# Two chained MLPs behind a Fourier transform: the first MLP cut into blocks of 512, 512 and 482 token pairs instead of 376

## The chip, the core and the metric

One core of a Trainium2 chip runs one program in one launch. The metric is the time of one execution on the device in microseconds (us). The kernel before takes 953.21 us, the median of three runs that lie between 952.99 and 953.53 us.

The core has five engines with a queue each, worked off in order: PE (TensorE) multiplies matrices and adds up in PSUM, DVE (VectorE) and POOL (GpSimd) do elementwise work, ACT (ScalarE) does functions and copies, and SP issues the DMA transfers between the core's memory and HBM. An instruction waits until semaphores say that its inputs are there and its output's buffer is free.

## The reference

```
x: (2, 3008, 256)
a = real(fft(fft(x, axis=1), axis=2))          # real part of the 2-D transform
a = a.reshape(6016, 256)
h = a @ moe_w_in                               # (256, 2048)
a = max(h, 0)**2 @ moe_w_out                   # (2048, 256)
h = a @ moe2_w_in
out = (h * sigmoid(1.702 * h)) @ moe2_w_out
```

All of it is in float32.

## The kernel before

**Token pairs.** The transform of real data gives token k and token 3008 - k almost the same inputs: one is the sum and the other the difference of an even and an odd part. The kernel works on pairs of tokens. Each batch has 1506 pairs, in four parts of frequencies of 378, 376, 376 and 376 pairs (`WID`); the kernel calls them `kb` 0 to 3.

**Words in two halves.** Every float32 matrix of the two MLPs is held as a high half and a low half in a shorter format (`float32r`), and a product is three matmuls: high by high, low by high, high by low. So each operand passes through a cast (high half, ACT, `H` or `h`) and a subtraction (low half, POOL or DVE, `G` or `l`). The weights come as 64-bit words and pass through six or seven integer and float operations first (operations i0A to u3l).

**The start.** The input arrives in six pieces f0 to f5 (three per batch). A piece is folded on DVE (`a`, `s`, `p`, `m`, `u`), goes through the transform over features on PE (`E`, `O`; lines 567 to 577, called L575 in the profile), is copied out by ACT (`e0`, `e1`, `o`), and the transform over positions makes from three pieces the four parts of a batch: `e00`, `e01` (even frequencies) and `o0` (the two odd parts) on PE at L624. PE is kept running with 24 matmuls on zeros (`WARM`, L469) before the first piece is there.

**The first MLP** runs over 8 blocks, one per part and batch, by 16 slices of 128 hidden units: 128 steps. A step i has five operations. `F` (L748 to L750): six matmuls into PSUM, for the even and the odd half. `P` (L1038 to L1041): three DVE instructions that form the two tokens of each pair and add the middle feature. `R` (L1049, L1050): relu and square, two ACT instructions, or one on DVE. `H` (L1055): the high half on ACT. `G` (L212): the low half on POOL or DVE. `B` (L763): twelve matmuls that add to four PSUM tiles, two per output half `ec` and token of the pair. So a step has 18 matmuls, each as wide as the block (376 or 378 columns). `X` takes a partial result out of PSUM to HBM and `Y` brings it back, since the first three blocks are worked in turns while the weights still arrive (`turns`, L733).

**The second MLP** runs over six blocks of 512, 512, 512, 512, 512 and 452 pairs, by 8 units of two slices: 48 units. The product with the first weight is done with seven products of half matrices in place of eight (21 matmuls, L1094), and the second with 24 (L1110): 45 matmuls in a unit. Its inputs come back from HBM (`load_y`); a block of 512 is put together from two or three blocks of the first MLP.

**Order.** The order of the operations up to the end of the first MLP is written out in `ORDER`, a list of names; what engine does an operation that may go to several is in `HOME`, and which buffer of a ring it takes in `RINGS`. The second MLP is written as a loop (L1119 to L1193) with `products`, `back2` and `leave`. After it, the last PSUM tile is copied out by ACT (L1198) and DVE (L1200), each half with its own DMA.

**Rings.** `LAG` (L736) is the number of steps whose `B` is left for the second MLP's first units. The rings of the first MLP hold 5 tiles `h`, 5 `gh`, 4 `gl` and 2 `p`.

Of the kernel before, what the change touches and what calls it, by code (L numbers as in the profile page):

```python
# [44 lines left out]
F4 H2 P4 o0s0 o0E1 o0c1
F5 u0l G1 R3 o0s1 P5 H3 R4 u1A i1S o02h
F6 B0 P6 i1O R5 B1 u1L R6 H4 G2 G3 H5 B2 i2D o02l u1C G4
F7 i1P o02N H6 o02n P7 G5 B3
F8 X3.0 P8 R7 X3.1 i1M u1O
F9 u2D i1N B4 P9 R8  # L50
F10 H7 i1H B5 H8
F11 G6 R9 P10 G7 i1l P11 u1S G8 R10 H9 B6
F12 G9 H10 f3D B7
F13 G10 R11 X7.0 P12 u1P i2A X7.1 R12 H11 u1H i2C
F14 G11 i2L B8 u1l H12 P13 B9 G12 R13 B10 u2A
F15 i2O B11 H13 P14 i2S
F16 R14 P15 i2P
F17 G13 H14 P16 i3D B12 R15 H15 G14 R16 P17
F18 i2M B13 R17 G15
F19 P18 u2C B14 H16 B15 i2N H17 G16 i2H R18 G17 i2l P19 u2L H18 R19 X15.1 X15.0 i3A  # L60
# [1271 lines left out]
```

## Time and profile before

| | |
|---|---|
| median of three runs | 953.21 us |
| the profiled execution: time, span of its records | 953.02 us, 950.8 us |
| PE busy | 942.8 us (99% of the span) |
| DVE, ACT, POOL busy | 686.0, 588.8, 280.2 us |
| HBM read and written | 37.36 MB and 15.42 MB |

The span is the time from the first to the last record; what lies around it in that execution is 2.2 us. Matmuls are pipelined: one shows some 335 ns from start to end while the next begins after about half of that. So the price of a matmul in a stream is read from the starts of two matmuls and the number between them, not from its duration.

### The profile page before, as it was taken

The numbers are of one execution on the slowest core, as the hardware profiler recorded it, in microseconds if no ns is written. First come the engines' busy times: TensorE is split into PE (matmuls) and PEld (weight loads), VectorE is DVE, ScalarE is ACT, GpSimd is POOL, SyncE is SP. The second block draws the span as 40 slices with busy tenths as digits, with TensorE's granted clock in tenths as the row PEclk, the third lists the DMA queues.
The fourth block names the chain that finished last, engine by engine and source line by source line (L and its number), as shares of the span: only waits on it lengthen the run. The fifth ranks groups of instructions, "written<-read, shape, count | busy, mean of one in ns | idle before, by whom it ended". The sixth has DMA issues, their size and how long they took to land.

```text
span 950.8 us, 12392 instructions
## 1 busy us (share of the span) xinstructions
PE 942.8 (99%) x4844; PEld 849.8 (89%) x4844; DVE 686.0 (72%) x902; ACT 588.8 (62%) x699; POOL 280.2 (29%) x171
## 2 busy tenths in 40 slices
PE   8999999999999999999999999999999999999997
PEld 8799999999999899999888888888888888888996
DVE  6899999887887787778797755665575575556553
ACT  3999997858587467867765644644454454455443
POOL 0655674424463367377105110030030002000000
PEclk9999999999999999999999999999999999999999
DMA  7442504221021010020330110020011001000001
GB/s 286 139 166 77 204 34 151 94 66 70 1 77 45 34 45 33 1 70 8 105 105 1 45 45 0 1 89 1 1 45 44 1 19 66 1 1 22 23 1 40
DMA packets 21898, 53.58 MB, mean 56 GB/s; under 512 B 3280, under 2 KB 15184, under 8 KB 19152
## 3 DMA queue, kind: packets, MB, share of 16 engines
q1 hardware_dynamic: 21840, 52.79, 15.8%
q8 instruction: 38, 0.62, 0.3%
q14 instruction: 20, 0.16, 0.1%
HBM read 37.36 MB, written 15.42 MB: 56 GB/s over the span
## 4 chain that ended last, share of the span: by engine, by line
PE 95%; DVE 2%; DMA 1%; ACT 1%; POOL 1%; issue 0%; SPq 0%; DVEq 0%; POOLq 0%
PE psb L763 27%; PE psb L1110 27%; PE psc L1094 24%; PE psa L748 4%; PE psa L749 4%; PE psa L750 4%; PE psa L624 2%; PE psb L624 1%; PE psa L575 1%; DMA xt<-in_x 1%; POOL gl L212 0%; PE psb L575 0%; DVE t L516 0%; DVE t L512 0%; DVE gl L212 0%
## 5 line engine op out<-in xcount | busy, mean ns | idle before, releaser
L763 PE MATMUL psb<-gh,w 128*128 128x376 f32 (+1 forms) x1024 | 233.6, 335 | 0.0
L212 POOL TENSOR_TENSOR gl<-h,gh 128x752 fp32r<-128x752 f32 (+1 forms) x91 | 176.7, 1949 | 161.1 <-ACT gh L1055 73.7
L763 PEld LDWEIGHTS psb<-gh,w 128*128 128x128 f32 x1024 | 181.6, 189 | 1.9 <-issue 1.2
L1110 PE MATMUL psb<-gh,w 128*128 128x512 f32 (+1 forms) x576 | 163.7, 386 | 0.0
L1174 DVE TENSOR_TENSOR g<-u,psc 128x1024 f32<-128x1024 f32 (+1 forms) x48 | 57.5, 1199 | 116.3 <-PE psc L1094 116.3
L1055 ACT CAST gh<-h 128x752 fp32r<-128x752 f32 (+1 forms) x128 | 103.1, 818 | 45.1 <-PE psb L763 44.3
L763 PE MATMUL psb<-gl,w 128*128 128x376 f32 (+1 forms) x512 | 129.8, 334 | 0.0
L1176 ACT ACTIVATE g<-g 128x1536 f32<-128x1536 f32 (+1 forms) x48 | 70.4, 1467 | 94.1 <-DVE g L1174 94.1
L1110 PEld LDWEIGHTS psb<-gh,w 128*128 128x128 f32 x576 | 108.1, 188 | 20.6
L212 DVE TENSOR_TENSOR gl<-g,gh 128x2048 fp32r<-128x2048 f32 (+1 forms) x48 | 109.0, 2270 | 1.5 <-ACT gh L1151 1.5
L1049 ACT ACTIVATE h<-h 128x752 f32<-128x752 f32 (+1 forms) x110 | 91.4, 831 | 21.7 <-DVE h L1041 19.7
L879 POOL TENSOR_TENSOR ue<-raw 128x512 f32<-128x512 f32 (+1 forms) x12 | 24.2, 2037 | 255.0 <-DMA raw<-ydram 248.7
L1050 ACT ACTIVATE h<-h 128x752 f32<-128x752 f32 (+1 forms) x110 | 91.9, 836 | 3.5
L1040 DVE TENSOR_TENSOR h<-p,psa 128x376 f32<-128x376 f32 (+1 forms) x128 | 70.0, 547 | 33.3 <-POOL gl L212 16.1
L763 PEld LDWEIGHTS psb<-gl,w 128*128 128x128 f32 x512 | 92.5, 188 | 0.0
L1038 DVE SCALAR_TENSOR_TENSOR p<-n,w1n_t,psa 128x376 f32<-128x376 f32 (+1 forms) x128 | 76.8, 600 | 20.2 <-PE psa L750 20.0
L1151 ACT CAST gh<-g 128x2048 fp32r<-128x2048 f32 (+1 forms) x48 | 90.2, 1878 | 0.3 <-ACT g L1176 0.3
L1110 PE MATMUL psb<-gl,w 128*128 128x512 f32 (+1 forms) x288 | 87.7, 386 | 0.0
L748 PE MATMUL psa<-eo,w 128*128 128x376 f32 (+1 forms) x256 | 86.4, 338 | 0.3 <-DVE n L306 0.3
L749 PE MATMUL psa<-eo,w 128*128 128x376 f32 (+1 forms) x256 | 85.7, 335 | 0.0
L750 PE MATMUL psa<-eo,w 128*128 128x376 f32 (+1 forms) x256 | 85.4, 334 | 0.0
L1173 ACT ACTIVATE g<-psc 128x512 f32<-128x512 f32 (+1 forms) x48 | 28.4, 591 | 77.7 <-PE psc L1094 77.7
(165 smaller groups left out, 1527.1 us busy)
## 6 DMA issues: line engine op xcount, KB each, us to landing
ydram<-o SPq DMA_DIRECT2D x17, 376.0 KB, 2.9
xt<-in_x SPq DMA_DIRECT2D x5, 1024.0 KB, 7.1
out<-o SPq DMA_DIRECT2D x10, 512.0 KB, 2.6
cst<-in_dfts SPq DMA_DIRECT2D x8, 570.0 KB, 6.0
raw<-in_w1i SPq DMA_DIRECT2D x4, 1024.0 KB, 5.0
raw<-in_w1o SPq DMA_DIRECT2D x4, 1024.0 KB, 6.2
raw<-in_w2i SPq DMA_DIRECT2D x4, 1024.0 KB, 5.3
raw<-in_w2o SPq DMA_DIRECT2D x4, 1024.0 KB, 5.1
```

Source lines behind the costliest of these rows:

```text
L212: eng.tensor_tensor(out=o, in0=a, in1=f32(b), op=ALU.subtract)
L748: T.matmul(o, lhsT=w[:, 0, fs], rhs=t[:, par, 0, 0:wd], start=True, stop=False)
L749: T.matmul(o, lhsT=w[:, 0, fs], rhs=t[:, par, 1, 0:wd], start=False, stop=False)
L750: T.matmul(o, lhsT=w[:, 1, fs], rhs=t[:, par, 0, 0:wd], start=False, stop=True)
L763: T.matmul(acc[j][ec][:, s, 0:wd], lhsT=w[:, hl, e0:e0 + P], rhs=(gh, gl)[gi][:, s, 0:wd], start=(first and hl == 0 and gi == 0), stop=(la ...
L1038: V.scalar_tensor_tensor(out=p[:, 0:wd], in0=e128[blocks[j]][:, 0:wd], scalar=w1n_t[:, 0, f:f + 1], in1=ps[:, 0, 0:wd], op0=ALU.mult, op1= ...
L1049: A.activation(out=hv, in_=hv, func=AF.Relu)
L1050: A.activation(out=hv, in_=hv, func=AF.Square)
L1055: A.copy(st["gh"][:, :, 0:wd], st["h"][:, :, 0:wd])
L1094: T.matmul(bank, lhsT=w[:, hl, slot * P:(slot + 1) * P], rhs=x[:, yl, 0:wd], start=(first and hl == 0 and yl == 0), stop=(hl == 1), skip_g ...
L1110: T.matmul(o[:, s, 0:wd], lhsT=w[:, hl, e0:e0 + P], rhs=g[:, 2 * i + s, 0:wd], start=(f == 0 and hl == 0 and g is gh), stop=(f == 15 and h ...
L1151: A.copy(gh, gs[u - 1])
```

## The change

What it does, part by part.

1. The 1506 pairs of a batch are cut into three blocks of 512, 512 and 482 (`WB`), whatever part they come from. The first MLP has 6 blocks and 96 steps. Block 0 holds part 0 and 134 pairs of part 1; block 1 the other 242 of part 1 and 270 of part 2; block 2 the other 106 of part 2 and part 3. So `h`, `l`, `m`, `n` of parts that are cut write two tiles (`e01hb`, `o02lb`, ...).
2. The second MLP has the same six blocks, 512, 512, 482 twice, and loads each with one DMA.
3. `LAG` is 3 and not 4; the rings hold 4 `h`, 4 `gh`, 3 `gl`. `ORDER`, `HOME` and `RINGS` are new.
4. The first input piece comes in two halves that are each contiguous, and is folded and transformed by halves (`f0p`, `f0pb`, `part_half`). The negated feature constants are no longer loaded, but made by ACT.
5. In the second MLP's last unit the matmuls on low halves stand last for the first output half, and for the second one all of token 0 stand before all of token 1. The last copies are three: token 0 by ACT, token 1 by DVE (240 columns) and ACT (242), into tiles and DMAs of their own.

```
-NP = 378
+NP = 512
+WB = [512, 512, 482]
...
-ORDER = """
-f0D dfD f0a1 f0a0 f0s0 nD f0p f0E f0s1 nyD seD ny f1D f0m f1s0 f2D f1a0 i0D f0e1 nA f1m f0O u0D c00D f1p f0o nC f1u i0A
...
+f0D nyD ny f0Db dfD f0a0 f0s0 f0p f1D nD f0m df f0a1 f0s1 f0pb f0E f0mb f2D f0O f1a0 i0D f1s0 u0D f1p f0Ob f1m f0Eb f1u
...
+TURNS = [(0, 0, 4), (1, 0, 4), (2, 0, 8), (1, 4, 12), (0, 4, 16), (1, 12, 16), (2, 8, 16)] + [(j, 0, 16) for j in range(3, 6)]
-PAIRS = B * sum(WID)
-WID2 = [min(NP2, PAIRS - NP2 * m) for m in range(BLKS)]
+WID2 = B * WB
...
-        nc.sync.dma_start(consts["dft"], dftd.rearrange("p (s l) -> p s l", s=2))
+        nc.sync.dma_start(consts["dft"][:, 0], dftd)
+
+    @op("df")
+    def _():
+        A.mul(consts["dft"][:, 1], consts["dft"][:, 0], -1.0)
...
+        def part_half(par, half):
...
+            for s, of_s in enumerate(slots()):
+                o = ps[:, s // 2, (s % 2) * 130:(s % 2) * 130 + 130] if par == 0 else ps[:, 0, s * P:(s + 1) * P]
+                for i, (v, j, minus, at) in enumerate(of_s):
+                    if at == half:
+                        T.matmul(o, lhsT=v[:, par, j], rhs=consts["dft"][:, minus, cols],
+                                 start=(not half and i == 0 and s in ((0, 2) if par == 0 else (0,))),
+                                 stop=(i == len(of_s) - 1), skip_group_check=True)
...
+    def block_parts(kb):
+
+        at = sum(WID[:kb])
+        for i in range(NC):
+            lo, hi = max(at, NP * i), min(at + WID[kb], NP * i + WB[i])
+            if lo < hi:
+                yield i, lo - at, hi - at, lo - NP * i
...
-    LAG = 4
+    LAG = 3
...
-        return [m.tile([P, 2, NP], F32, **of("h", 5), name="ht") for _ in range(2)]
+        return [m.tile([P, 2, NP], F32, **of("h", 4), name="ht") for _ in range(2)]
...
-        for j, lo, hi, at in pieces(m):
-            nc.sync.dma_start(yr[m][:, :, :, at:at + hi - lo], ydram[j][:, :, :, lo:hi])
+        nc.sync.dma_start(yr[m][:, :, :, 0:WID2[m]], ydram[m][:, :, :, 0:WID2[m]])
...
-            st["gh"] = mg.tile([P, 2, NP], F32R, **of("gh", 5), name="gh")
+            st["gh"] = mg.tile([P, 2, NP], F32R, **of("gh", 4), name="gh")
...
-            gl = mg.tile([P, 2, NP], F32R, **of("gl", 4), name="gl")
+            gl = mg.tile([P, 2, NP], F32R, **of("gl", 3), name="gl")
...
+        terms = [(i, hl, g, s) for i in range(2) for hl, g in ((0, gh), (0, gl), (1, gh)) for s in range(2)]
+        if u == units - 1:
+            terms.sort(key=(lambda x: x[3]) if ec else (lambda x: x[2] is gl))
...
-        A.copy(o[:, 0, 0:wd], acc["2", BLKS - 1][1][:, 0, 0:wd])
-        nc.sync.dma_start(out[BLKS - 1, 1, :, 0, 0:wd], o[:, 0, 0:wd])
-        V.tensor_copy(o[:, 1, 0:wd], acc["2", BLKS - 1][1][:, 1, 0:wd])
-        nc.sync.dma_start(out[BLKS - 1, 1, :, 1, 0:wd], o[:, 1, 0:wd])
+        at = wd // 4 * 2
+        o1, o2 = (m2.tile([P, NP2], F32, tag=tag, name="o") for tag in ("a1", "u"))
+        for eng, to, s, lo, hi in ((A, o1, 0, 0, wd), (V, o2, 1, 0, at), (A, o[:, 0], 1, at, wd)):
+            copy(eng, to[:, lo:hi], acc["2", BLKS - 1][1][:, s, lo:hi])
+            nc.sync.dma_start(out[BLKS - 1, 1, :, s, lo:hi], to[:, lo:hi])
```

Three places of the new order, on the engines themselves. The first is PE's queue ahead of the first MLP step: `psa` and `psb` are PSUM tiles, `zc` and `zs` the transformed pieces, `cst` the constants of positions, `eo` the block that a step reads. Before, from the transform for part 0 to the first step:

```order
22 L624 MATMUL psa<-cst,zs 128x189
23 L624 MATMUL psa<-cst,zs 128x189 [waits Activation_49]
24 L624 MATMUL psa<-cst,zs 128x189 x2
25 L624 MATMUL psb<-cst,zc 128x189 x4
26 L624 MATMUL psb<-cst,zc 128x188 [waits DMAHW3_49,PE_49]
27 L624 MATMUL psb<-cst,zc 128x188 x3
28 L624 MATMUL psb<-cst,zs 128x188 x4
29 L748 MATMUL psa<-eo,w 128x378 [waits Activation_49]
30 L749 MATMUL psa<-eo,w 128x378 [waits DVE_49]
```

And in the changed kernel:

```order
24 L644 MATMUL psa<-cst,zs 128x189
25 L644 MATMUL psa<-cst,zs 128x189 [waits Activation_49] x2
26 L644 MATMUL psa<-cst,zs 128x189
27 L644 MATMUL psb<-cst,zc 128x188 [waits DMAHW3_49,PE_49]
28 L644 MATMUL psb<-cst,zc 128x188 x3
29 L644 MATMUL psb<-cst,zs 128x188 x4
30 L644 MATMUL psb<-cst,zc 128x188 x4
31 L644 MATMUL psb<-cst,zc 128x189 [waits DVE_49,Activation_49]
32 L644 MATMUL psb<-cst,zc 128x189 x3
33 L771 MATMUL psa<-eo,w 128x512 [waits Activation_49]
34 L772 MATMUL psa<-eo,w 128x512 [waits DVE_49]
```

The middle feature of part 1 (four matmuls, row 30) has come ahead of the first step, and that of part 0 (rows 31 and 32) behind part 1, where it waits for DVE and ACT to free a PSUM tile.

The second place is ACT's queue at the same time: `zc` and `zs` are the copies `e0`, `e1`, `o`, and `ue` is a weight on its way. Before:

```order
14 L596 ACTIVATE zc<-psa,nyq 128x65 [waits PE_49]
15 L596 ACTIVATE zc<-psa,nyq 128x65 x3
16 L497 CAST sel_t<-sel_raw 128x128
17 L306 COPY zs<-psb 128x512
18 L596 ACTIVATE zc<-psa,nyq 128x65 x4
19 L596 ACTIVATE zc<-psa,nyq 128x65 [waits PE_49]
20 L596 ACTIVATE zc<-psa,nyq 128x65 x3
21 L306 COPY zs<-psb 128x512 [waits PE_49]
22 L319 ACTIVATE ue<-raw 128x1024 [waits DMAHW1_49,DVE_49]
```

And in the changed kernel:

```order
15 L598 ACTIVATE zc<-psa,nyq 128x65 [waits PE_49]
16 L598 ACTIVATE zc<-psa,nyq 128x65 x3
17 L289 ACTIVATE ue<-raw 128x1024 [waits DMAHW2_49,DMAHW0_49,DVE_49]
18 L598 ACTIVATE zc<-psa,nyq 128x65 [waits PE_49]
19 L598 ACTIVATE zc<-psa,nyq 128x65 x7
20 L467 COPY mask<-sel_raw 128x1 [waits DMAHW2_49]
21 L471 CAST sel_t<-sel_raw 128x128
22 L276 COPY zs<-psb 128x512 [waits PE_49]
23 L276 COPY zs<-psb 128x512
24 L295 ACTIVATE ue<-raw 128x1024
```

A conversion of a weight (row 17) has come between the copies of the third piece, and both `zs` copies stand at the end.

The third place is the end of the program, ACT and DVE. ACT before, its last five instructions:

```order
670 L1173 ACTIVATE g<-psc 128x452 [waits DVE_49,PE_49]
671 L1176 ACTIVATE g<-g 128x3x452 [waits DVE_49]
672 L1151 CAST gh<-g 128x4x452 [waits PE_49,Activation_49]
673 L1116 COPY o<-psb 128x2x452 [waits DMAHW1_49,DMAHW0_49,PE_49]
674 L1198 COPY o<-psb 128x452 [waits DVE_49,PE_49]
```

ACT in the changed kernel:

```order
604 L1188 ACTIVATE g<-g 128x3x482 [waits DVE_49]
605 L1163 CAST gh<-g 128x4x482 [waits PE_49,Activation_49]
606 L1128 COPY o<-psb 128x2x482 [waits DMAHW6_49,DMAHW5_49,PE_49]
607 L276 COPY o<-psb 128x482 [waits PE_49]
608 L276 COPY o<-psb 128x242 [waits DVE_49]
```

DVE in the changed kernel:

```order
793 L1155 TENSOR_TENSOR g<-g,psc 128x482 [waits DVE_49]
794 L1186 TENSOR_TENSOR g<-u,psc 128x2x482 [waits PE_49]
795 L180 TENSOR_TENSOR gl<-g,gh 128x4x482 [waits Activation_49]
796 L180 TENSOR_TENSOR gl<-g,gh 128x4x482 [waits DVE_49,Activation_49]
797 L276 COPY o<-psb 128x240 [waits Activation_49]
```

The last copies have become three, and each still names the other engine as what it waits for: DVE's waits for ACT, and ACT's second for DVE.

## Rows read from the trace of the kernel before

**Rows 1.** The page: span, busy shares, and the chain that ended last by engine.
```profile
span 950.8 us, 12392 instructions
...
PE 942.8 (99%) x4844; PEld 849.8 (89%) x4844; DVE 686.0 (72%) x902; ACT 588.8 (62%) x699; POOL 280.2 (29%) x171
...
PE 95%; DVE 2%; DMA 1%; ACT 1%; POOL 1%; issue 0%; SPq 0%; DVEq 0%; POOLq 0%
```

**Rows 2.** Timeline of PE, first MLP, 376 columns: start, length, operation, count.
```profile
362.41 0.33 PE L748 MATMUL psa<-eo,w 128*128 128x376 f32 x1
...
374.82 0.51 PE L763 MATMUL psb<-gh,w 128*128 128x376 f32 x2
```

**Rows 3.** Timeline of PE, second MLP, 512 columns.
```profile
702.41 2.20 PE L1094 MATMUL psc<-yc,w2i 128*128 128x512 f32 x9
...
712.61 2.20 PE L1094 MATMUL psc<-yc,w2i 128*128 128x512 f32 x9
```

**Rows 4.** Timeline of PE, second MLP, 452 columns.
```profile
891.62 0.57 PE L1110 MATMUL psb<-gh,w 128*128 128x452 f32 x2
...
900.92 0.37 PE L1110 MATMUL psb<-gh,w 128*128 128x452 f32 x1
```

**Rows 5.** Busy time by stretch: length, PE, PEld, DVE, ACT, POOL, granted clock, DMA.
```profile
40.00:80.00 40.00, 40.00 (x226) 37.64 (x223) 37.16 (x60) 37.98 (x49) 25.03 (x13) 1.00 0.32 118
80.00:120.00 40.00, 40.00 (x234) 40.00 (x233) 36.71 (x57) 36.87 (x46) 25.43 (x13) 1.00 0.43 147
```

**Rows 6.** Groups by line and shape: count, busy us, mean ns, idle before.
```profile
L212 POOL TENSOR_TENSOR gl<-h,gh 128x752 fp32r<-128x752 f32 x67 | 129.6, 1942 | 125.3 <-ACT gh L1055 61.9 <-PE psb L763 23.4 <-PE psa L750 10.3
...
L1049 ACT ACTIVATE h<-h 128x752 f32<-128x752 f32 x82 | 68.1, 830 | 18.8 <-DVE h L1041 17.1 <-POOL gl L212 1.7
...
L1040 DVE TENSOR_TENSOR h<-p,psa 128x376 f32<-128x376 f32 x96 | 52.4, 546 | 25.4 <-POOL gl L212 12.3 <-DMA ydram<-o 2.8 <-DVE p L1038 1.3
...
L1141 DVE TENSOR_TENSOR u<-a,psc 128x512 f32<-128x512 f32 x40 | 27.4, 685 | 37.6 <-ACT a L1138 37.6
```

**Rows 7.** Timeline of PE at the start, idle time before a row in brackets.
```profile
1.05 8.51 PE L469 MATMUL psa<-still 128*128 128x128 f32 x48 [1.05 <-DVE still L292]
10.44 2.95 PE L575 MATMUL psa<-dft,xt 128*128 128x130 f32 x24 [0.89 <-DVE xt L531]
...
16.96 2.05 PE L575 MATMUL psa<-dft,xt 128*128 128x130 f32 x16 [0.89 <-DVE xt L542]
...
21.28 2.05 PE L575 MATMUL psa<-dft,xt 128*128 128x130 f32 x16
...
26.22 1.43 PE L624 MATMUL psa<-cst,zs 128*128 128x189 f32 x8
...
31.64 0.44 PE L748 MATMUL psa<-eo,w 128*128 128x378 f32 x1
...
33.83 1.31 PE L624 MATMUL psb<-cst,zc 128*128 128x188 f32 x8
```

**Rows 8.** Timeline of ACT at the start.
```profile
23.95 1.79 ACT L596 ACTIVATE zc<-psa,nyq 128x65 f32<-128x65 f32 x8
25.54 0.68 ACT L306 COPY zs<-psb 128x512 f32<-128x512 f32 x1
...
30.36 1.16 ACT L319 ACTIVATE ue<-raw 128x1024 f32<-128x1024 f32 x1
```

**Rows 9.** The end: timelines of PE, ACT, DVE and SP, and the last transfers.
```profile
936.47 0.68 PE L1110 MATMUL psb<-gl,raw 128*128 128x452 f32 x2 [0.24 <-DVE gl L212]
...
946.27 0.54 ACT L1198 COPY o<-psb 128x452 f32<-128x452 f32 x1 [1.57 <-PE psb L1110]
...
946.84 0.63 DVE L1200 COPY o<-psb 128x452 f32<-128x452 f32 x1 [6.88 <-ACT o L1198]
...
947.49 0.33 SPq L1201 DMA_DIRECT2D out<-o  x1
...
out<-o SPq DMA_DIRECT2D x2, 226.0 KB, 2.3
```

More of the change, by code (lines that the diff above doesn't have):

```diff
@@ L45 @@
[L45 to L60, printed above, removed]
@@ L506, in fold, with _ @@
         b, c = divmod(q, NC)
-        ops[f"f{q}D"] = lambda: load_x(q)
+        @op(f"f{q}D")
+        def _():
+            first, *others = load_x(q)
+            first()
+            for x in others:
+                ops[f"f{q}Db"] = x
         whole = once(lambda: xp.tile([P, 2, 8, P], F32, tag="t", name="t", bufs=1))
@@ L563, in slots @@
             else:
-                even = [[(gv[:, :, i], j, s * i) for i in range(2) for j in range(2)] for s in range(2)]
+                even = [[(gv[:, :, i], j, s * i, i) for i in range(2) for j in range(2)] for s in range(2)]
+                return even + [[(gv[:, :, j], 0, 0, j), (gv[:, :, j], 1, 1, j)] for j in range(2)]
             return even + [[(gv[:, :, j], 0, 0), (gv[:, :, j], 1, 1)] for j in range(2)]
+        def part_half(par, half):
+            if not half:
+                held[par] = ps_b() if f"f0{'EO'[par]}" in IN_B else ps_a()
+            ps = held[par]
+            cols = slice(0, 130) if par == 0 else slice(130, 258)
+            if par == 0 and not half:
+                keep_busy(ps[:, 0, 384:512], WARM[q])
+            for s, of_s in enumerate(slots()):
[5 more added lines that the diff above has]
+                                 stop=(i == len(of_s) - 1), skip_group_check=True)
         def part(name, par):
@@ L577, in part @@
                              skip_group_check=True)
-        ops[f"f{q}E"] = lambda: part(f"f{q}E", 0)
-        ops[f"f{q}O"] = lambda: part(f"f{q}O", 1)
+        if q == 0:
+            for par in range(2):
+                for half in range(2):
+                    ops[f"f0{'EO'[par]}" + "b" * half] = lambda par=par, half=half: part_half(par, half)
+        else:
+            ops[f"f{q}E"] = lambda: part(f"f{q}E", 0)
+            ops[f"f{q}O"] = lambda: part(f"f{q}O", 1)
         def z(t, n):
@@ L680, in _ @@
         def _():
[L681 to L683 removed]
+            for at, f in ((0, ALU.add), (hw, ALU.subtract)):
+                for i, lo, hi, to in block_parts(kb):
+                    lo2, hi2 = max(lo, at), min(hi, at + hw)
+                    if lo2 < hi2:
+                        V.tensor_tensor(out=n_tile(NC * b + i)[:, to + lo2 - lo:to + hi2 - lo], in0=held["a"][:, lo2 - at:hi2 - at],
+                                        in1=held["n"][:, 1, lo2 - at:hi2 - at], op=f)
     def odd_k(b, make):
@@ L753, in back @@
     def back(j, f, first, last, ecs=range(2)):
-        wd = WID[blocks[j][1]]
+        wd = WB[j % NC]
         if first:
@@ L831, in _ @@
             def _():
-                leaving[j] = [m.tile([P, 2, NP], F32, **of("h", 5), name="o") for _ in range(2)]
+                leaving[j] = [m.tile([P, 2, NP], F32, **of("h", 4), name="o") for _ in range(2)]
                 for ec, o in enumerate(leaving[j]):
@@ L839, in _ @@
                 ap = acc[j][ec][:, :, 0:wd]
-                o = (leaving[j][ec] if last else m.tile([P, 2, NP], F32, **of("h", 5), name="o"))[:, :, 0:wd]
+                o = (leaving[j][ec] if last else m.tile([P, 2, NP], F32, **of("h", 4), name="o"))[:, :, 0:wd]
                 if last:
```

362 lines of the change are left out of this document (173 added, 189 removed).

## The prediction

> **What bounds the kernel now.** I read the page first: PE is busy for 942.8 us of a span of 950.8, and 95% of the chain that ended last is PE [rows 1]. So of the span only 8 us are not PE's, most of them ahead of the first real matmul and behind the last one. Then the busy time by stretch: from 40 to 120 us PE is busy for all 80 us at a granted clock of 1.00, the level of 2.4 GHz, while ACT has 74.9 us of work there and DVE 73.9 [rows 5]. The reader is to see two things in this: the time is the sum of the prices of the matmuls, and two other engines stand at 92 to 94% behind it, so that little may go wrong with them. Last the timelines, for the price of a matmul and for both ends of the program.
>
> **The price of a matmul** is read from starts. From 362.41 to 374.82 us PE starts 72 matmuls of 376 columns: 12.41/72 = 0.1724 us each [rows 2]. From 702.41 to 712.61 it starts 45 of 512 columns, one unit of the second MLP: 0.2267 us each [rows 3]. From 891.62 to 900.92 it starts 45 of 452: 0.2067 us [rows 4]. A column at 2.4 GHz is 0.4167 ns, so 376, 452 and 512 columns are 156.7, 188.3 and 213.3 ns, and what comes on top of each matmul is 15.7, 18.3 and 13.3 ns. That piece belongs to the matmul and not to its columns, and fewer, wider matmuls pay it less often.
>
> The Trainium skill (TensorE: Matmul & The Clock Gate, Back-to-back issue gap) gives an isolated gap between matmuls of N/2.4 ns and some 2.5 ns, a much smaller piece. By its figure the estimate of what the wider blocks save would be 576 matmuls less by 2.5 ns, 1.4 us. The rows disagree with it, with 13 to 18 ns for these operands, and the sum goes by the rows.
>
> **The change, part by part.**
>
> *Blocks of the first MLP.* Before, 16 slices of 18 matmuls, 288, each by two blocks of 378 and six of 376. All at the price of 376: 288 x 8 x 0.1724 = 397.2 us. After, 288 x (4 x 0.2267 + 2 x p), p the price of 482 columns, which no row shows. Bounds: with the 13.3 ns of 512 it is 0.2142; the dearest reading is a pattern that fits the rows, columns rounded up to 16 and 32 cycles more (464 + 32 = 496 cycles is 452's 0.2067, 544 is 512's 0.2267; 376's would be 416 for a measured 414), and gives 528 cycles, 0.2200. A straight line between 452 and 512 gives 0.2167. I take the overhead of 452, the nearest width that isn't a full tile: 200.8 + 18.3 = 0.2192. Then after is 288 x 1.3452 = 387.4 us: 9.8 us less (12.7 and 9.3 less at the bounds).
>
> *Blocks of the second MLP.* 48 units of 45 matmuls, 360 of them per block. Before 360 x (5 x 0.2267 + 0.2067) = 482.5 us, after 360 x (4 x 0.2267 + 2 x 0.2192) = 484.3: 1.8 us more (1.8 less and 2.3 more at the bounds). The other engines have room there: that stretch is not among those where ACT is full.
>
> *What else rides on a step.* DVE, ACT and POOL pay per instruction too, so wider tiles don't hurt them: a DVE sum out of PSUM takes 546 ns at 376 columns and 685 at 512, a factor of 1.25 for 1.36 the columns [rows 6]. P, three such, goes from 1.64 to 2.06 us, while a step on PE goes from 18 x 0.1724 = 3.10 to 4.08. R and H on ACT are three instructions of 0.83 us [rows 6], 2.49; after at most 1.36 times that, 3.39, for the 4.08. So their share of a step does not grow, and the cover that hides them stays.
>
> *Rings and LAG.* From F to B a step goes P, R, H, G: 1.64 + 2.49 + 1.94 [rows 6] = 6.1 us before, in 4 steps of 3.10, 12.4: 6.3 us of slack. After, 2.06 + 3.39 + 2.64 (POOL's 1.94 by 1.36) = 8.1 in 3 steps of 4.08, 12.2: 4.1 us. I expect the slack to do, since before no PE wait shows in either stretch [rows 5], but a queue that is 94% full may now eat it here and there: between 0 and 3 us, and I take 0.5.
>
> *The start.* PE runs zeros to 9.56 us, then waits twice for folds, 0.89 us each [rows 7]. Halves make the first fold short, so both can go: the transform of the third piece would end 1.8 us earlier, at 21.4 in place of 23.2. But what follows is ACT's, and longer than before: behind that piece stand four `zc` copies (half of 1.79), a weight's conversion (1.16), eight more (1.79), two small ones (some 0.3) and two `zs` copies of 0.68 [rows 8], 5.5 us, less some 0.6 by which ACT's instructions overlap: 26.3 to 26.7. Two PE instructions of part 0 stand behind the last `zs`, 0.7 us by the row of 1.43 for four [rows 7], so part 0 ends at 27.4, where it ended at 26.22 + 1.35 = 27.6 before. Then part 1's eight instructions, 2.7, to 30.1. Part 0's middle feature must wait for ACT's copy and DVE's two sums to free its tile, 1.5 us, and takes 1.3: 32.9. The first step needs both parts now, and its low half ends at about 33.4. Before, it started at 31.64 with 1.31 us of part 1's middle feature still to come [rows 7], so 32.95 for the same work. I take a loss of 0.4 us; the bounds are 1.0 us gained, if ACT's chain is shorter, and 2.0 lost, if DVE, which has the conversions of two weights there, adds to it.
>
> *The end.* Before, PE waits 0.24 us for a low half in the last unit [rows 9]; six more matmuls of about 0.2 us now stand ahead of the low ones, and the wait goes: 0.24 less. The split of the last copies does not do what its shape says. DVE's copy, before, stood idle until ACT's of the same PSUM tile had ended [rows 9], and in the new order it still waits for ACT and for nothing of PE's. It reads what the last matmul wrote, so ACT's first copy must itself wait for the last matmul, and ACT's second waits for DVE. So three copies follow each other: 0.57 (0.54 by 482/452), about 0.38 and about 0.36 (the row of 0.63 by the columns, and its fixed part), 1.31 us for 1.17 before [rows 9]. The last transfer is half as large; of its 2.3 us [rows 9] I take 0.1 off. Sum 0, between 0.4 less and 0.4 more; with copies that did run beside each other it would be 0.7 less.
>
> *Sum.* -9.8 + 1.8 + 0.5 + 0.4 - 0.24 + 0 = -7.3 us, against the profiled execution's 953.02: 945.7. That execution lies 0.2 under the median of the runs, 953.21; I say 945.6.
>
> **The rivals.**
>
> *The price of 482 is that of a full tile.* If the 13.3 ns of 512 holds for 482, the blocks bring -12.7 - 1.8 and all else +0.7: 953.0 - 13.8 = 939.2. For it: 512 is the only width of the new kernel with a row. Against it: 452, also not a full tile, has 18.3.
>
> *The overhead is not per matmul.* If what comes on top of the columns in the first MLP were no piece of each matmul but a share of the columns (15.7 of 156.7 ns, a tenth, for any width there), 576 matmuls less bring nothing, and the rest of the sum is left, +0.7 with the second MLP unchanged: 953.7, no change that can be told. Against it stand the rows of 452 and 512, where the piece does not grow with the width. The rule of the Trainium skill named above, with its 1.4 us, would also end here, at about 952.
>
> *The shorter slack stalls PE (the other side).* Place: the stretch of 40 to 120 us, where ACT and DVE are at 92 to 94% and the weights are still being converted; some 20 of the new steps lie in it. If the chain from F to B is late by x at each, PE idles 20x. The kernel gets slower from 20x = 7.3 + 1.9, x = 0.46 us, on; at x = 0.7 the time is 945.7 + 14 - 0.5 = 959. For it: slack falls from 6.3 to 4.1 us and each ring by one. Against it: a ring of 4 wide tiles holds 4 x 4.08 = 16.3 us of work, one of 5 held 15.5, and PE lost nothing there before.
>
> **How the numbers follow.** A measurement of this kernel can tell 0.2%, 1.9 us, from no change: faster is under 951.3, slower over 955.1. The forecast, with its own range of 942 to 949 (the start, the stalls and the upper price bound), has 0.68; 482 at a full tile's price, 936.5 to 942, 0.16; partial stalls, 949 to 951.3, 0.08; no piece to save, about 953, 0.03; stalls of about 3 to 9 us more, within 1.9 us of before, 0.02; slower, 0.03. So faster is 0.68 + 0.16 + 0.08 = 0.92, same 0.05, slower 0.03. The range 938.5 to 950 leaves out the ends of both.
>
> **What would show it.** PE's busy time should fall by about 8 us, to 935. Starts of 45 matmuls of 512 in the first MLP should lie 10.2 us apart; those of 482 columns give p, with 0.2192 forecast and 0.2142 and 0.2200 at its ends. The first step should start near 33 us, with an idle time of about 0.5 to 1 us in PE between the third piece and part 0, released by ACT. At the end ACT's first copy should start only behind the last matmul, and the three copies follow each other. PE should show no idle time above 1 us from 40 to 440 us; waits for POOL's or DVE's `gl`, for ACT's `gh` or for DVE's `h` that add up to over 3 us would be the stall rival. The forecast is wrong if PE's busy time falls by less than 5 or more than 15 us.

## The result and the profile after

The changed kernel takes 960.45 us, the median of four runs from 959.60 to 961.38; the kernel before, on the same chip, 953.10 (951.55 to 953.53). The ratio is 1.0079, with a 95% interval of 1.0067 to 1.0092: slower by 0.8%, where 945.6 was forecast and slower had a chance of 0.03.

The page of the changed kernel's profiled execution: the span, the busy time of each engine, and the chain that ended last.

```profile
span 959.4 us, 10948 instructions
PE 946.4 (99%) x4272; PEld 776.5 (81%) x4272; DVE 689.9 (72%) x801; ACT 582.2 (61%) x621; POOL 265.2 (28%) x146
...
PE 85%; DVE 6%; issue 1%; ACT 0%; POOL 0%; DVEq 0%; POOLq 0%; ACTq 0%
```

PE has 572 matmuls less and is busy 3.6 us longer than in [rows 1]; and the chain, which was PE's for 95%, now runs through DVE for 6% of the span. Two things went wrong, then: the price of a matmul, and waits for DVE.

**The price.** A timeline of PE in the first MLP, in a place where nothing waits (start, duration, line, operands, tile, count):

```profile
320.72 0.40 PE L771 MATMUL psa<-eo,w 128*128 128x512 f32 x1
...
322.12 0.63 PE L786 MATMUL psb<-gh,w 128*128 128x512 f32 x2
322.58 0.63 PE L786 MATMUL psb<-gl,w 128*128 128x512 f32 x2
...
324.92 0.40 PE L771 MATMUL psa<-eo,w 128*128 128x512 f32 x1
```

From 320.72 to 324.92 PE starts 18 matmuls of 512 columns, one step: 4.20/18 = 0.2333 us each. The second MLP's price for the same width is 0.2267 [rows 3], and PE shows no idle time in either stretch. The price of 482 columns is 0.2200 in both MLPs; in the first one, six take 1.32 us:

```profile
448.28 0.38 PE L771 MATMUL psa<-eo,w 128*128 128x482 f32 x1
...
449.60 0.38 PE L786 MATMUL psb<-gh,w 128*128 128x482 f32 x1
```

**The waits.** Busy time by stretch (us of each engine, instructions in brackets, granted clock, DMA share), to be held against [rows 5]; then what PE waited for longest:

```profile
40.00:80.00 40.00, 39.35 (x169) 29.96 (x168) 36.96 (x43) 33.86 (x37) 26.50 (x13) 1.00 0.26 89
80.00:120.00 40.00, 36.80 (x162) 29.65 (x161) 38.80 (x44) 31.10 (x32) 21.74 (x9) 1.00 0.19 64
120.00:160.00 40.00, 39.33 (x168) 30.93 (x167) 38.73 (x45) 31.80 (x33) 25.04 (x10) 1.00 0.41 144
```

```profile
PE psa L771 <- DVE h L1053: 1.9, 5, 0.4
PE psb L786 <- DVE o L276: 1.6, 1, 1.6
```

Columns after the length of the stretch are PE, its weight loads, DVE, ACT, POOL. PE was busy for all 80 us between 40 and 120 before, and is idle for 3.85 of them now; DVE went from 36.71 to 38.80 of 40 between 80 and 120. That table is even too kind, since a matmul's record runs on while the next could start: by the distances between starts, less the price of each, PE loses 7.0 us between 50 and 136 us, in nine places. The largest, on PE, DVE and POOL:

```profile
87.08 0.60 PE L786 MATMUL psb<-gh,w 128*128 128x482 f32 x2
89.29 0.71 PE L786 MATMUL psb<-gh,w 128*128 128x482 f32 x2 [1.61 <-DVE o L276]
```

```profile
75.11 1.22 DVE L313 SCALAR_TENSOR_TENSOR ue<-raw,ue 128x1024 uint32<-128x1024 uint32 x1
76.25 2.77 DVE L302 TENSOR_SCALAR ue<-ue 128x1024 f32<-128x1024 f32 x1
...
84.73 0.65 DVE L1053 TENSOR_TENSOR h<-p,psa 128x482 f32<-128x482 f32 x1
85.30 2.80 DVE L313 SCALAR_TENSOR_TENSOR ue<-raw,ue 128x1024 uint32<-128x1024 uint32 x1
88.02 1.21 DVE L276 COPY o<-psb 128x1024 f32<-128x1024 f32 x1
```

```profile
75.37 3.10 POOL L180 TENSOR_TENSOR gl<-h,gh 128x964 fp32r<-128x964 f32 x1 [2.78 <-ACT gh L1067]
...
84.74 2.27 POOL L180 TENSOR_TENSOR gl<-h,gh 128x964 fp32r<-128x964 f32 x1 [3.04 <-ACT gh L1067]
```

PE waits for a PSUM tile that DVE's copy (L276) empties, and that copy stands behind L313, a conversion of a weight, which took 2.80 us. The same instruction takes 1.22 at 75.11. It ends at 88.10, and the POOL instruction that ran when it began ends at 87.01: 1.09 us earlier, a little less than the time that L313 takes alone. L302, 0.68 at its shortest, does the same: 79.02 is 0.55 behind POOL's 78.47. Fifteen DVE instructions between 40 and 240 us are longer by over 0.2 us than the shortest of the same line and shape in that stretch. At every one a POOL instruction was running, and the end lies behind the end of a POOL instruction by 0.13 to 0.20 us less than the DVE instruction takes alone: 0.55 us for one operand of 1024 columns or two of 512 (0.69 and 0.75 alone), 1.02 to 1.10 for two operands of 964 or 1024 (1.16 and 1.22 alone). The excess adds up to 21.3 us; counted in the same way it is 7.0 in the kernel before. DVE's sums out of PSUM don't show it: L1053 at 84.73 takes its 0.65 us beside the POOL instruction of 84.74. So DVE looks busy while it waits inside its instruction. POOL is held in the same way when it comes second: its instruction of 75.37 begins while L313 runs, ends 2.14 us after it, and shows 3.10 us for work that takes 2.27 at 84.74.

The Trainium skill (SBUF — State Buffer, Who interferes with whom) states this as a lock: VectorE in its two-port modes, or with two operands in SBUF, and GpSimd share a pair of ports, and who comes second is blocked until the first one's instruction ends. The rows above agree with it, kind by kind.

**Start and end.** The first step begins at 31.99 with part 1's middle feature (28.89) already done; the same work stood at 31.64 + 1.31 = 32.95 before [rows 7]. At the end the three last copies follow each other:

```profile
28.89 1.42 PE L644 MATMUL psb<-cst,zc 128*128 128x188 f32 x8
30.66 1.40 PE L644 MATMUL psb<-cst,zc 128*128 128x189 f32 x8 [0.35 <-DVE ht L688]
31.99 0.50 PE L771 MATMUL psa<-eo,w 128*128 128x512 f32 x1
```

```profile
954.82 0.56 ACT L276 COPY o<-psb 128x482 f32<-128x482 f32 x1 [1.67 <-PE psb L1122]
955.86 0.36 ACT L276 COPY o<-psb 128x242 f32<-128x242 f32 x1 [0.47 <-DVE o L276]
```

with DVE's from 955.42 between them. From the last matmul's end to the span's end are 4.6 us, as before.

### The profile page after: what moved, and what is told of

Same layout as the page of the kernel before. It is cut to its first block, busy times and chain, and to the rows that moved or that the text cites. A ratio compares the mean times of both kernels' runs of the same rounds, so it can differ in the third digit from the quotient of the medians.

```text
span 959.4 us, 10948 instructions
## 1 busy us (share of the span) xinstructions
PE 946.4 (99%) x4272; PEld 776.5 (81%) x4272; DVE 689.9 (72%) x801; ACT 582.2 (61%) x621; POOL 265.2 (28%) x146
## 4 chain that ended last, share of the span: by engine, by line
PE 85%; DVE 6%; issue 1%; ACT 0%; POOL 0%; DVEq 0%; POOLq 0%; ACTq 0%
PE psb L1122 27%; PE psc L1106 23%; PE psb L786 23%; PE psa L771 4%; PE psa L773 4%; PE psa L772 4%; PE psa L644 2%; DVE ue L313 1%; DVE h L1053 1%; DVE h L1052 1%; DVE p L1050 1%; DVE ue L307 0%; PE psa L572 0%; DVE ue L319 0%; DVE ue L302 0%
## 5 line engine op out<-in xcount | busy, mean ns | idle before, releaser
L786 PE MATMUL psb<-gh,w 128*128 128x512 f32 (+1 forms) x768 | 220.2, 392 | 2.1 <-DVE o L276 1.6
L180 POOL TENSOR_TENSOR gl<-h,gh 128x1024 fp32r<-128x1024 f32 (+1 forms) x67 | 166.7, 2491 | 186.4 <-PE psb L786 81.4
L786 PEld LDWEIGHTS psb<-gh,w 128*128 128x128 f32 x768 | 143.1, 188 | 34.9 <-DVE o L276 2.0
L1122 PE MATMUL psb<-gh,w 128*128 128x512 f32 (+1 forms) x576 | 164.3, 387 | 0.0
L1067 ACT CAST gh<-h 128x1024 fp32r<-128x1024 f32 (+1 forms) x96 | 98.4, 1031 | 50.7 <-PE psb L786 43.1
L1122 PEld LDWEIGHTS psb<-gh,w 128*128 128x128 f32 x576 | 108.3, 188 | 21.0
L786 PE MATMUL psb<-gl,w 128*128 128x512 f32 (+1 forms) x384 | 118.9, 390 | 0.0
L1061 ACT ACTIVATE h<-h 128x1024 f32<-128x1024 f32 (+1 forms) x86 | 89.5, 1040 | 35.5 <-DVE h L1053 35.4
L1052 DVE TENSOR_TENSOR h<-p,psa 128x512 f32<-128x512 f32 (+1 forms) x96 | 65.1, 678 | 40.3 <-POOL gl L180 27.0
L1062 ACT ACTIVATE h<-h 128x1024 f32<-128x1024 f32 (+1 forms) x86 | 90.0, 1046 | 2.7
L1122 PE MATMUL psb<-gl,w 128*128 128x512 f32 (+1 forms) x288 | 88.1, 387 | 0.0
L786 PEld LDWEIGHTS psb<-gl,w 128*128 128x128 f32 x384 | 72.0, 188 | 15.8
L1050 DVE SCALAR_TENSOR_TENSOR p<-n,w1n_t,psa 128x512 f32<-128x512 f32 (+1 forms) x96 | 70.2, 731 | 15.2 <-PE psa L773 14.9
L771 PE MATMUL psa<-eo,w 128*128 128x512 f32 (+1 forms) x192 | 76.6, 399 | 2.9 <-DVE h L1053 1.9
L772 PE MATMUL psa<-eo,w 128*128 128x512 f32 (+1 forms) x192 | 75.1, 391 | 0.0
L773 PE MATMUL psa<-eo,w 128*128 128x512 f32 (+1 forms) x192 | 75.0, 390 | 0.0
```

Source lines behind the costliest of these rows:

```text
L180: eng.tensor_tensor(out=o, in0=a, in1=f32(b), op=ALU.subtract)
L771: T.matmul(o, lhsT=w[:, 0, fs], rhs=t[:, par, 0, 0:wd], start=True, stop=False)
L772: T.matmul(o, lhsT=w[:, 0, fs], rhs=t[:, par, 1, 0:wd], start=False, stop=False)
L773: T.matmul(o, lhsT=w[:, 1, fs], rhs=t[:, par, 0, 0:wd], start=False, stop=True)
L786: T.matmul(acc[j][ec][:, s, 0:wd], lhsT=w[:, hl, e0:e0 + P], rhs=(gh, gl)[gi][:, s, 0:wd], start=(first and hl == 0 and gi == 0), stop=(la ...
L1050: V.scalar_tensor_tensor(out=p[:, 0:wd], in0=e128[j][:, 0:wd], scalar=w1n_t[:, 0, f:f + 1], in1=ps[:, 0, 0:wd], op0=ALU.mult, op1=ALU.add)
```

## The experiments

Theory A: the price of a matmul depends on where its streamed operand starts in SBUF. By the addresses in the built program, all streamed operands of the first MLP (`gh`, `gl`, the halves `eo`) start 32 bytes past a multiple of 64 in the changed kernel, those of the second MLP at a multiple of 64; before, those of the first MLP lay at 0, 8, 16, 32, 40 and more, with 376 columns. The weights of both MLPs start at multiples of 64 in both kernels; theory A says nothing of them, and e11 below shows that it should. Theory B: POOL's instructions, longer now, hold DVE up, and DVE holds up PE. The rivals stand in the expectations. Ratios are to the kernel before, measured beside each run, with a 95% interval; beside them is the ratio's difference from 1, times 953 us. e3_shift32_nolow and e4_streams were run once and have no ratio.

| run | ratio | us |
|---|---|---|
| the changed kernel | 1.0079 (1.0067 to 1.0092) | +7.5 |
| e1_shift32 | 0.9995 (0.9984 to 1.0006) | -0.5 |
| e5_half | 1.0018 (1.0009 to 1.0027) | +1.7 |
| e6_nolow | 1.0006 (0.9997 to 1.0015) | +0.6 |
| e2_shift32_half | 0.9964 (0.9951 to 0.9977) | -3.4 |
| e7_before_nolow | 1.0003 (0.9994 to 1.0013) | +0.3 |
| e8_shift32_quarter | 0.9989 (0.9980 to 0.9998) | -1.0 |
| e9_half_relu_act | 0.9969 (0.9958 to 0.9980) | -3.0 |
| e10_half_tail | 0.9958 (0.9946 to 0.9971) | -4.0 |
| e11_before_off32 | 1.0074 (1.0057 to 1.0091) | +7.1 |

### e1_shift32

```
+    pad = tc.alloc_tile_pool(name="pad", bufs=1, side="right", reuse_waits="tile")
+    pad.tile([P, 8], F32, name="gap")
     mg = tc.alloc_tile_pool(name="mg", bufs=2, side="right", reuse_waits="tile")
```

> The changed kernel with 32 bytes left free above the buffers of the first MLP, so that every operand that its matmuls stream (gh, gl, and the halves of the inputs) starts at a multiple of 64 bytes and not 32 bytes past one; nothing else changes. Theory A (the price of a streamed matmul goes by the number of 64-byte pieces its operand lies in): a 512-column matmul of the first MLP falls from 0.2335 to 0.2267 us, as in the second MLP, 482 columns stay at 0.2200, and 1152 x 6.7 ns = 7.7 us go; where VectorE sets the pace (40 to 200 us) part of that comes back as idle time of PE: 952.7 to 956 us. Rival (the first MLP's 512 columns cost 0.2335 for another reason: PSUM, weight loads, the other engines): price and time unchanged, 960.4 us.

Measured: 951.47 us (950.05 to 955.49). A step of 512 columns without a wait on PE:

```profile
322.67 0.61 PE L788 MATMUL psb<-gh,w 128*128 128x512 f32 x2
323.12 0.62 PE L788 MATMUL psb<-gl,w 128*128 128x512 f32 x2
323.58 1.07 PE L788 MATMUL psb<-gh,w 128*128 128x512 f32 x4
324.49 0.62 PE L788 MATMUL psb<-gl,w 128*128 128x512 f32 x2
324.94 0.62 PE L788 MATMUL psb<-gh,w 128*128 128x512 f32 x2
325.39 0.39 PE L773 MATMUL psa<-eo,w 128*128 128x512 f32 x1
```

Twelve in 2.72 us, 0.2267 each, as in the second MLP. The price is back, as theory A says; 32 bytes of layout are worth 8 us by the ratios, 9 by the medians. That is more than 1152 x 6.7 ns = 7.7, and with the same order and the same POOL instructions DVE's stretched time fell too, from 21.3 to 9.4 us: what meets what depends on when things run. Nine of the twelve runs lie between 950.05 and 952.17 us and three between 954.83 and 955.49; the trace is of one of the nine, and what the three have in common isn't shown.

### e4_streams

```
+    for n, off in [(512, 0)] + STREAMS:
+        o = ps.tile([P, 512], F32, tag="o", name=f"n{n}at{off}")
+        for i in range(48):
+            k = i % 3
+            nc.tensor.matmul(o[:, 0:n], lhsT=w[:, k * P:(k + 1) * P], rhs=mv[:, off // 4:off // 4 + n],
+                             start=(i == 0), stop=(i == 47))
```

> PE alone: streams of 48 matmuls of one width and one start of the streamed operand, nothing else running (computes none of the reference). Theory A, one 16-column piece of 64 bytes in 16 cycles of 2.4 GHz and 32 cycles more: 512 columns 0.2267 us from start 0 and 0.2333 from 8, 16, 24, 32, 40, 48, 56 bytes; 482 columns 0.2200 from every start; 376 columns 0.1733 from 0 to 32 and 0.1800 from 40 to 56; 378 columns 0.1733 from 0, 0.1800 from 32 and 40; 452 0.2067 from both; 480 0.2133 and 0.2200; 496 0.2200 and 0.2267; 498 and 504 0.2267 from both. Rival (price by columns alone, start without effect): N/2.4 ns and some 13 ns: 512 0.2267, 504 0.2233, 498 0.2208, 496 0.2200, 482 0.2142, 480 0.2133, 452 0.2017, 378 0.1708, 376 0.1700 from every start.

Measured, from the starts of 48 matmuls to the start of the next stream, in us per matmul (columns of the table: bytes past a multiple of 64):

| columns | 0 | 8 | 16 | 24 | 32 | 40 | 48 | 56 |
|---|---|---|---|---|---|---|---|---|
| 512 | 0.2267 | 0.2335 | 0.2317 | 0.2331 | 0.2331 | 0.2335 | 0.2331 | 0.2304 |
| 504 | 0.2271 | | | | 0.2268 | | | |
| 498 | 0.2267 | | | | 0.2267 | | | |
| 496 | 0.2198 | | | | 0.2246 | | | |
| 482 | 0.2200 | | 0.2177 | | 0.2198 | | 0.2200 | 0.2198 |
| 480 | 0.2167 | | | | 0.2200 | | | |
| 452 | 0.2067 | | | | 0.2067 | | | |
| 378 | 0.1731 | | | | 0.1733 | 0.1733 | | |
| 376 | 0.1731 | 0.1733 | 0.1700 | 0.1733 | 0.1731 | 0.1731 | 0.1731 | 0.1733 |

How two of them are read, 512 columns from 0 and from 32 bytes (the trace drops the digits at the end of a name):

```profile
18.23 10.14 PE L30 MATMUL n512at<-mv,w 128*128 128x512 f32 x44
...
62.65 10.42 PE L30 MATMUL n512at<-mv,w 128*128 128x512 f32 x44
```

44 matmuls, the last of which shows 0.39 us: 9.75/43 = 0.2267 and 10.03/43 = 0.2333. PE does this alone, with no other engine at work. So the dearer price is PE's own and goes by the start of the streamed operand, for 512 columns at every start but 0. The weights start at a multiple of 64 in all of these streams, so this run can't tell the operand's own start from its distance to the weights. Theory A's exact rule, 16 cycles for each piece of 64 bytes that is touched and 32 more, missed: 376 and 378 columns touch one more piece from 40 bytes and cost the same, 480 from 0 costs 520 cycles and not 512, 496 from 32 bytes lies between. The price by columns alone, the rival, missed by more.

### e11_before_off32

```
+    gap = ctx.enter_context(tc.tile_pool(name="gap", bufs=1))
+    gap.tile([P, 8], F32, name="gap")
     winp = ctx.enter_context(tc.tile_pool(name="winp", bufs=4))
```

> The kernel before with 32 bytes left free below its buffers on the left, so that 1160 of its 512-column matmuls of the second MLP (680 on m2, 240 each on two weight buffers that hold inputs) stream an operand that starts 32 bytes past a multiple of 64; 640 others, the 452 and the first MLP's 376 columns stay as they were or cost the same from any start. Nothing else changes. Theory A: 1160 x 6.7 ns = 7.8 us, 961 us, and 512 columns at 0.2333 us from those buffers beside 0.2267 from the others in one unit. Rival (the start of the operand matters in the changed kernel's first MLP alone, or not by itself): 953 us.

Measured: 959.37 us (958.64 to 959.57), 7.1 more, close to the 7.8 expected; but the dear matmuls are not those that were expected. The rows show two units of the second MLP. Counted from the end they are the 26th and the 25th last, so by the kernel's code `gh` lies on the left in the first of them (m2, moved, like the weights and `ya`, `yb`, `yc`) and on the right in the second (m3, not moved, like `gl` in both):

```profile
702.93 0.62 PE L1112 MATMUL psb<-gh,raw 128*128 128x512 f32 x2
703.39 0.63 PE L1112 MATMUL psb<-gl,raw 128*128 128x512 f32 x2
703.86 1.07 PE L1112 MATMUL psb<-gh,raw 128*128 128x512 f32 x4
704.77 0.63 PE L1112 MATMUL psb<-gl,raw 128*128 128x512 f32 x2
...
711.85 1.52 PE L1096 MATMUL psc<-ya,w2i 128*128 128x512 f32 x6
713.21 0.63 PE L1112 MATMUL psb<-gh,raw 128*128 128x512 f32 x2
713.68 0.63 PE L1112 MATMUL psb<-gl,raw 128*128 128x512 f32 x2
714.15 1.09 PE L1112 MATMUL psb<-gh,raw 128*128 128x512 f32 x4
715.08 0.63 PE L1112 MATMUL psb<-gl,raw 128*128 128x512 f32 x2
```

What was moved is cheap: `ya`, six in 1.36 us, 0.2267 each, and `gh` in the first unit, four in 0.91. What stayed at a multiple of 64 is dear: `gl`, two in 0.47, and `gh` in the second unit, four in 0.93. Over all units the 1160 matmuls that were to become dear take 0.2279 us on average, and the 640 that were to stay cheap 0.2338. So theory A fails in the form in which it was expected to hold here, and the sum of 1160 x 6.7 ns came near the time by luck: by the starts, all 1800 take 5.7 us more than before, 4.5 of it in the 640; the rest falls on the first few matmuls behind a dear run, which take up to 0.236 us. What fits this run and the others is the distance between the streamed operand and the weights: 0.2267 where both start at a multiple of 64 or both 32 bytes past one, 0.2333 where one of them is 32 bytes off the other. In the changed kernel it was the operand that stood off, here it is the weights. Why the distance matters is not shown. The rival (no effect in the kernel before) is refuted: 32 empty bytes made it almost as slow as the changed one.

### e5_half and e2_shift32_half

```
-            sub(on(f"G{i}", "G"), gl[:, :, 0:wd], st["h"][:, :, 0:wd], gh[:, :, 0:wd])
+            eng = on(f"G{i}", "G")
+            for s in (slice(0, 1), slice(1, 2)) if eng is G else (slice(0, 2),):
+                sub(eng, gl[:, s, 0:wd], st["h"][:, s, 0:wd], gh[:, s, 0:wd])
```

> The changed kernel with its operands where they were (32 bytes past a multiple of 64), and GpSimd's low halves of the first MLP in two instructions of one token each. Theory B (VectorE waits for the end of a running GpSimd instruction, and PE for VectorE): stretched VectorE time between 40 and 240 us falls from 21.3 to 12 us or less, PE's idle time from 40 to 240 us from 5.3 to 3 us or less, 957 to 958.5 us. Rival (the 1.7 us that the same edit gave beside the shifted operands is not GpSimd's doing): 960 us.

> As e1_shift32, and GpSimd's low halves in the first MLP are made by two instructions of one token each (512 or 482 columns) in place of one of both. Theory B (PE's waits between 40 and 240 us come from VectorE instructions that wait until a running GpSimd instruction ends, 21.3 us of stretched VectorE time in the changed kernel against 7.0 before): the longest wait is halved, stretched time falls to about 10 us, PE's idle time there (5 to 6 us) falls to 2 to 3 us, and the time is 2 to 4 us under e1_shift32. Rival (VectorE is simply full there, or the shorter rings set the waits): same time as e1_shift32, within 1 us, or more, since GpSimd pays its fixed cost twice.

Measured: 955.00 us (953.87 to 956.08) without the shift and 949.74 (948.48 to 950.44) with it. By the ratios that is 5.8 us less than the changed kernel for the halves alone, and 3 us less than e1_shift32 (1.7 by the medians). In e5_half, stretched DVE time falls to 12.5 us, and PE works through all 120 us in which it lost 4.5:

```profile
40.00:80.00 40.00, 40.00 (x176) 30.96 (x173) 36.93 (x49) 34.66 (x39) 30.35 (x21) 1.00 0.29 96
80.00:120.00 40.00, 40.00 (x180) 33.42 (x179) 36.06 (x45) 35.75 (x37) 25.75 (x18) 1.00 0.28 93
120.00:160.00 40.00, 40.00 (x173) 32.15 (x172) 38.12 (x47) 33.23 (x34) 29.29 (x19) 1.00 0.47 177
```

By the starts, PE's loss between 50 and 136 us falls from 7.0 to 0.1 us. Theory B is borne out: the waits go when POOL's instructions are shorter, with the same rings and `LAG`, though POOL is busy longer (25.75 for 21.74). More was won than was expected, 955.0 for 957 to 958.5. e2_shift32_half is a version that beats both kernels.

### e6_nolow, e3_shift32_nolow and e7_before_nolow

```
+            if on(f"G{i}", "G") is G and i < 40:
+                gl = gh
+            else:
+                gl = mg.tile([P, 2, NP], F32R, **of("gl", 3), name="gl")
+                sub(on(f"G{i}", "G"), gl[:, :, 0:wd], st["h"][:, :, 0:wd], gh[:, :, 0:wd])
```

> The changed kernel with its operands where they were, without GpSimd's low halves in steps 0 to 39 of the first MLP (that part of the computation is left out; the matmuls stream the high half in its place). Theory B: the whole price of GpSimd's instructions to VectorE and so to PE, 955 to 956.5 us, with PE idle under 1 us between 40 and 240 us; the prices of the matmuls stay at 0.2335 us for 512 columns. Rival (other causes): above 958.5 us.

> As e1_shift32, but in steps 0 to 39 of the first MLP where GpSimd makes the low half it isn't made (that part of the computation is left out), and the matmuls stream the high half in its place. PE's matmuls are the same in number and width. Theory B: no GpSimd instruction holds VectorE up there but those on weights; stretched VectorE time between 40 and 200 us falls under 6 us and PE's idle time there under 1.5 us; the time is 4 to 6 us under e1_shift32. Rival (VectorE has too much to do there whatever GpSimd does): PE's idle time stays at 4 us or more and the time within 1.5 us of e1_shift32.

> The kernel before without GpSimd's low halves in its steps 0 to 52 (left out as in e6_nolow; the same stretch of time). Theory B with the change as its cause: before, PE does not wait there, so nothing is to be had: 952.5 to 953.2 us, though stretched VectorE time falls from 7.0 to under 3 us. Rival (GpSimd's instructions cost the kernel before as much as the changed one): 948.5 to 949.5 us.

Measured: e6_nolow 953.59 us (953.11 to 954.16), 6.9 under the changed kernel; e3_shift32_nolow 947.48 in one run; e7_before_nolow 953.49 (952.42 to 953.93), which can't be told from the kernel before (its stretched time fell from 7.0 to 4.9 us, not under 3). In e6_nolow stretched DVE time is 1.8 us, L313 and L302 take their 1.22 and 0.70 us in the place shown above, and PE waits for no DVE instruction of the first MLP:

```profile
70.99 1.22 DVE L313 SCALAR_TENSOR_TENSOR ue<-raw,ue 128x1024 uint32<-128x1024 uint32 x1
72.17 0.70 DVE L302 TENSOR_SCALAR ue<-ue 128x1024 f32<-128x1024 f32 x1
...
79.44 1.22 DVE L313 SCALAR_TENSOR_TENSOR ue<-raw,ue 128x1024 uint32<-128x1024 uint32 x1
```

```profile
PE psb L572 <- DVE xt L522: 1.3, 1, 1.3
PE psa L439 <- DVE still L262: 1.1, 1, 1.1
PE psc L1109 <- DVE g L1158: 0.5, 1, 0.5
PE psb L644 <- DVE ht L688: 0.3, 1, 0.3
PE psb L1125 <- DVE gl L180: 0.3, 1, 0.3
```

So POOL's instructions cost the changed kernel 7 us, all the waits that it has there, with `LAG` 3 and the short rings of `h` and `gh` in place; they cost the kernel before nothing that can be told. e6 alone would leave a rival: without the low halves the ring of `gl` is not used either, and no matmul waits for them. But the changed kernel's list of waits has none of PE for POOL's `gl`, and in e5, where that ring is in use, the waits are gone too. From e6_nolow to the one run of e3_shift32_nolow it is the price again, 6.1 us of the 7.7 that 1152 x 6.7 ns gives.

### e8_shift32_quarter

```
+            cuts = (0, 256, wd) if eng is G else (0, wd)
...
+            for s in (slice(0, 512), slice(512, 1024)) if on(name + "l", "G") is G else (slice(0, 1024),):
+                sub(on(name + "l", "G"), w[:, 1, s], ue()[:, spot, s], w[:, 0, s])
```

> As e2_shift32_half, with GpSimd's low halves in four instructions (256 and 256 or 226 columns of one token) and its low halves of weights in two. Theory B: each wait of VectorE falls to a GpSimd instruction of some 0.8 us and its own time; if GpSimd's added fixed cost (some 0.3 us an instruction, by 283 against 265 us busy) makes no low half late, 948 to 949 us, under e2_shift32_half. Rival (what is left is not VectorE's waiting, or GpSimd is late then): 949.7 us or more.

Measured: 951.80 us (950.84 to 952.95), 2 more than with halves. A miss: stretched time is 12.9 us in 22 instructions (11.3 in 18 with halves), and PE is idle for 2.9 us between 80 and 240 us. There are more stretched instructions, and POOL pays per instruction (306.8 us busy for 265.2 in the changed kernel). The two edits of this run were not told apart.

### e9_half_relu_act and e10_half_tail

```
-HOME = {... "f3s0 i3l j0L o0c1 R3 G4 ... G11 R15 i2l ... f5o R42 G41 R44 e11c ..." "V"}
+HOME = {... "f3s0 i3l j0L o0c1 G4 ... G11 i2l ... f5o G41 e11c ..." "V"}
```

```
-        if u == units - 1:
-            terms.sort(key=(lambda x: x[3]) if ec else (lambda x: x[2] is gl))
...
-        for eng, to, s, lo, hi in ((A, o1, 0, 0, wd), (V, o2, 1, 0, at), (A, o[:, 0], 1, at, wd)):
-            copy(eng, to[:, lo:hi], acc["2", BLKS - 1][1][:, s, lo:hi])
-            nc.sync.dma_start(out[BLKS - 1, 1, :, s, lo:hi], to[:, lo:hi])
+        A.copy(o[:, 0, 0:wd], acc["2", BLKS - 1][1][:, 0, 0:wd])
+        nc.sync.dma_start(out[BLKS - 1, 1, :, 0, 0:wd], o[:, 0, 0:wd])
+        V.tensor_copy(o[:, 1, 0:wd], acc["2", BLKS - 1][1][:, 1, 0:wd])
+        nc.sync.dma_start(out[BLKS - 1, 1, :, 1, 0:wd], o[:, 1, 0:wd])
```

> As e2_shift32_half, with relu and square of steps 3, 15, 42 and 44 on ScalarE (two instructions of 1.0 us each) and not on VectorE (one of 1.3 to 2.2 us). Theory C (what still idles PE between 40 and 240 us is VectorE's work, of which this takes off 6 us): PE's idle time there falls from 1.2 to under 0.5 us and the time is 0.5 to 1 us under e2_shift32_half. Rival (ScalarE, 34 of 40 us busy there, is as full): the same within 0.5 us, or slower, with waits of PE on ScalarE's h.

> As e2_shift32_half, with the end of the kernel before: the last unit's matmuls in the old order and two last copies, one per token, in place of three. By the prediction's term for the end (0: the three copies follow one another as the two did): the same time within 0.5 us, and the span ends 4.6 us after the last matmul as it does with three. Rival (the split end is worth its 0.5 us or more either way): the time moves by more than 0.5 us.

Measured: 950.41 us (948.54 to 951.83) and 949.45 (948.16 to 949.70). Neither can be told from e2_shift32_half. Taking four relus off DVE brings nothing: its stretched time rises to 14.6 us, and theory C has no support. The old end is as good as the split one, and the span ends 4.6 us after the last matmul with either.

## Why the prediction was wrong

By its own steps, on the profiled spans (959.4 against 950.8, 8.6 more, where the sum said 7.3 less):

- **The price of 512 columns in the first MLP** was taken from a row of the second MLP. This term failed: 0.2333 and not 0.2267, for 288 x 4 = 1152 matmuls, +7.7 us. No bound was set on it, since the width had a row; what the row did not say is where that operand starts, and where its weights start. e1, e4 and e11 show it.
- **Rings and LAG**, +0.5 with a bound of 3. This step failed too: PE loses 7.0 us between 50 and 136 us, +6.5. It was a wait of the kind that the rival on the other side named, in the place that it named, and at 959 that rival had the time nearly right, by luck: it took 14 us of stalls, twice what came, and had no dearer price. Its mechanism, the slack from F to B and the shorter rings, was not it. With the same rings and `LAG` the waits are gone when POOL's low halves are cut in two (e5). What was missed stands in "what else rides on a step": POOL's instruction was scaled as work of POOL's (1.94 us to 2.64 estimated, 2.50 measured at 1024 columns, 2.41 where nothing holds it), and not as time in which DVE is held.
- **The price of 482 columns**: 0.2200, the upper bound, for 0.2192 taken; 1296 matmuls, +1.0. The pattern that gave the bound holds for 376, 452, 482 and 512, and fails at 480.
- **The second MLP**: by these prices +2.3, the upper bound given; with it one wait of 0.55 us for DVE at 474.62, which was not in the sum.
- **The start**: -1.0 us, the lower bound, for +0.4 taken. Right in the range; 1.4 us better than the value taken.
- **The wait for the low half** was to go; PE still waits 0.26 us, at 944.41. Wrong, +0.2. The row was misread: counted from the end, the wait stands in the last unit but one before as after, and the new order is that of the last unit alone.
- **The end**: 0, and the three copies follow one another by the mechanism that the prediction gave. Right, and e10 agrees.
- **Not in the sum**: the matmuls of the transforms and of the middle features, some in two pieces now, with what is lost between them, take some 1.5 us more from the first step on.

Together -7.3 + 7.7 + 6.5 + 1.0 + 0.6 - 1.4 + 0.2 + 1.5 = +8.8 for a measured +8.6. What the prediction said of blocks is right where its price holds: with 0.2267 as in e1_shift32, and without POOL's low halves in the way (e3_shift32_nolow, which leaves them out), 947.48 us were measured in one run, 1.9 above the forecast.

PE's busy time was to fall by 8 us and rose by 3.6; that was the sign named for a wrong forecast. 45 matmuls of 512 columns take 45 x 0.2333 = 10.5 us in the first MLP, not 10.2.

What stays open: why the distance between operand and weights has a price; and how much of POOL's effect comes from its longer instruction, how much from the new order, in which it meets DVE's conversions more often, and how much from buffers with less reserve. e1_shift32 has the same order and half the stretched time, so chance has a part.
